# Linear attention with a gated feed-forward: activation tables chosen from sets, guard sums taken on VectorE, and a new order list

## The chip, the cores and the metric

The kernel runs on one core of a Trainium2 chip. The metric is the device time of one execution in microseconds (us). The engines of the core are TensorE (PE; its weight loads are shown apart as PEld), VectorE (DVE), ScalarE (ACT), GpSimd (POOL) and SyncE (SP, which here issues every DMA).

## The reference, cut to what matters

```
mag = sqrt(a_re² + a_im²);  scale = min(mag, 0.999) / (mag + 1e-6)
S[t] = (a[t]·scale[t]) * S[t-1] + k[t] v[t]^T        # complex decay per row of S, 48 x 48 a head
y[t] = q[t] · Re S[t]                                # 4 batches, 8 heads, 768 steps, 48 wide
x = y, heads side by side                            # 4 x 768 x 384
h = relu(x @ w_in)                                   # 384 -> 1024
c = sum over k of conv_w[k] * h shifted by k-1       # along the sequence, 3 taps
out = (h * sigmoid(c)) @ w_out                       # 1024 -> 384
```

## The kernel before, in words

The recurrence is rewritten as chunked attention. The sequence of each batch is cut into 6 chunks of 128 steps, 24 in all. Decays are summed as logarithms and phases along the sequence, so that q and k can be scaled by exp of the summed logarithm and turned by cosine and sine of the summed phase; what is left is a masked product of the two inside a chunk, and a state that is carried from chunk to chunk.

Work comes in 12 segments of two chunks. For each segment:

- `prelude` (L291) loads a_re and a_im (768 columns each) into the tile a_t, squares both on ACT (L300, L301, each with a sum along the row into one column of `gar` or `gai`), adds the squares on DVE (L302), takes logarithms and exponentials on ACT (L303 to L308), the quotient on DVE (L309), and a running sum on DVE (L312, three scans of 256). Then come the arctangent on ACT (L316), a running sum of the phase (L318, three scans), its turns as whole numbers (an ACT copy recorded at the helper's L281), their removal on DVE (L325) and an absolute value (L327).
- `products` (L329) loads q and k (tile qk_t) and v (v_t), takes two exponentials on ACT (L337, L338), scales k and q (L339, L340), takes cosine and sine on ACT (L344, L345; the function Sin), and multiplies on DVE (L346, L347, L348). The results are laid out head by head in two `stk` tiles by 16 DMAs (L353): eight from qk_t, which wait for L347, and eight from a_t, which wait for L348. SP issues them.
- For each chunk, `state` (L363) transposes on PE (L373), copies to `kn` on ACT (L374), multiplies (L380) and copies the state to `s_sb` (L387). `attention` (L390) computes scores on PE (L398), masks them on DVE (L401, tile p_t), and multiplies by state and values (L411). The result is copied to the tile `x` in two parts, on ACT (L423) and DVE (L424); a column at a unit's border is copied on ACT by `halo` (L431, recorded at L281).

The feed-forward works on 9 units of 256 or 384 steps, with four steps each of 256 hidden channels. `moe_front` (L464) has 18 matmuls into h_ps (L477), Relu on ACT (L480) and two convolution taps on DVE (L481, L483). `moe_back` (L486) has tanh on ACT (L495), the gate on DVE (L496), a two-part copy on ACT (L498) and DVE (L499), and the matmuls into o (L504); after the fourth step ACT copies o to os_t (L510) and SP stores it. At the start, w_in, w_out and conv_w arrive in a 64-bit layout and are turned into fp32 on DVE (L239 to L242), split into two parts on ACT (L272, L278) with PE's help (L276, L277).

At the end a few small DVE operations (L542 to L551) test the guard sums `gar` and `gai` against 4096 and other values against limits; where a limit is broken, a slow path (`recurrence`) runs. On these inputs it is not run.

The order of all of this is not left to the program text. `pieces` cuts the program into 1761 pieces (one instruction, or a run of PE instructions with the same target); `in_order` (L164) sorts them by the hand-written list `RANKS` (L45) and ties each engine's instructions into that one line. Each engine, and SP's queue, works strictly in that line's order. While it does so, it puts an activation table load (recorded at L181) in front of an ACT instruction whose function is not served by the table loaded last:

```
"Exp": (natural_log_exp,), "Ln": (natural_log_exp,), "Sin": (silu,), "Arctan": (sigmoid,), "Tanh": (sigmoid, silu)
need = table_of(row[0])
if need and table not in need:
    table = need[0]; row = [load of table, *row]
```

Squares, copies, Relu and Abs name no table and never cause a load.

Of the kernel before, what the change touches and what calls it, by code (L numbers as in the profile page):

```python
# [126 lines left out]
]  # L127

HINT = "TileBranchHintPlaceholder"
HINTED = {"EngineType.PE": 10, "EngineType.DVE": 1, "EngineType.Activation": 2, "EngineType.SP": 2, "EngineType.Pool": 0}  # L130

# [568 lines left out]
```

## Time and profile before

| what | us |
|---|---|
| median of 3 runs | 398.24 |
| lowest and highest | 397.48, 400.33 |
| the profiled execution's own time | 399.31 |
| its span, first to last instruction | 397.5 |
| ACT_TABLE_LOAD, 41 in all (40 of them by `in_order`) | 1.283 each |

The profile is of one execution. The span leaves out 1.8 us that lie around the instructions. Busy shares are of the span; a PE that is shown busy is not always at its peak, since its ends are modelled.

### The profile page before, as it was taken

What the parts mean: (1) busy time and instruction counts of PE and PEld (TensorE: products, weight loads), DVE (VectorE), ACT (ScalarE), POOL (GpSimd) and SP (SyncE); (2) the same over time, 40 slices, a digit from 0 to 9 for tenths busy, and PEclk for the clock granted to TensorE, in tenths of its full rate; (3) what the DMA queues carried; (4) which work ended last, traced back from release to release, by engine and by line L of the source; (5) the groups of instructions that cost most, each with busy time, mean ns of one, the idle gap of its engine ahead of it and who ended that gap; (6) DMA issues with size and microseconds to landing.
All of it is one profiled execution on the core that took longest, in us unless ns stands there. A gap on an engine that the chain in (4) does not pass through costs nothing. (4 is left out here: it accounts for less than half of the span.)

```text
span 397.5 us, 10141 instructions
## 1 busy us (share of the span) xinstructions
PE 359.7 (90%) x4146; PEld 326.6 (82%) x4146; DVE 334.6 (84%) x505; ACT 342.8 (86%) x602; POOL 4.0 (1%) x33
## 2 busy tenths in 40 slices
PE   1455696999999999999999989999999999999994
PEld 1123365899999999999989979999999999999994
DVE  3799976799999999999989977989999877862880
ACT  4999998899999999999998989999999887640751
POOL 2000000000000000000000000000000000000000
PEclk9997579799999999999999999999999999999999
DMA  8983678258774754692468823852718605500102
GB/s 300 419 326 103 103 170 224 91 119 195 201 184 147 146 145 120 130 228 75 89 103 239 190 96 101 145 193 87 137 25 183 164 2 103 119 2 2 59 0 70
DMA packets 31495, 55.03 MB, mean 138 GB/s; under 512 B 4304, under 2 KB 25808, under 8 KB 31440
## 3 DMA queue, kind: packets, MB, share of 16 engines
q1 hardware_dynamic: 31440, 54.31, 52.6%
q8 instruction: 34, 0.56, 0.6%
q14 instruction: 21, 0.17, 0.1%
HBM read 30.70 MB, written 4.72 MB: 89 GB/s over the span
## 5 line engine op out<-in xcount | busy, mean ns | idle before, releaser
L504 PE MATMUL o<-wo,hg 128*128 128x384 f32 x576 | 116.0, 345 | 0.0
L477 PE MATMUL h_ps<-x,wi 128*128 128x386 f32 (+1 forms) x648 | 113.0, 325 | 0.0
L477 PEld LDWEIGHTS h_ps<-x,wi 128*128 128x128 f32 x648 | 103.2, 189 | 1.7 <-issue 0.8
L504 PEld LDWEIGHTS o<-wo,hg 128*128 128x128 f32 x576 | 97.9, 188 | 2.6 <-issue 1.4
L398 PE MATMUL ps<-stk 96*128 96x128 f32 x384 | 52.4, 286 | 1.9 <-DMA stk<-a_t 1.7
L398 PEld LDWEIGHTS ps<-stk 96*128 96x128 f32 x384 | 49.7, 200 | 4.0 <-issue 2.7
L181 ACT ACT_TABLE_LOAD x40 | 51.3, 1283 | 0.7
L481 DVE SCALAR_TENSOR_TENSOR g_t<-h_t,cw 128x384 f32<-128x384 f32 (+1 forms) x72 | 39.9, 568 | 8.3 <-ACT h_t L480 8.0
L495 ACT ACTIVATE g_t<-g_t,cw 128x384 f32<-128x384 f32 (+1 forms) x72 | 39.5, 576 | 2.5 <-DVE g_t L483 2.5
L483 DVE SCALAR_TENSOR_TENSOR g_t<-h_t,cw,g_t 128x384 f32<-128x384 f32 (+1 forms) x72 | 39.5, 567 | 0.5
L480 ACT ACTIVATE h_t<-h_ps 128x386 f32<-128x386 f32 (+1 forms) x72 | 31.7, 452 | 8.8 <-PE h_ps L477 8.4
L401 DVE TENSOR_TENSOR p_t<-ps,mask 128x512 f32<-128x512 f32 x48 | 32.7, 683 | 6.9 <-PE ps L398 6.8
L276 PE MATMUL h_ps<-g_t,ident 128*128 128x384 f32 x32 | 21.9, 800 | 17.3 <-DVE g_t L242 9.6
L499 DVE TENSOR_TENSOR hg<-g_t,hg 128x768 fp32r<-128x768 f32 (+1 forms) x36 | 31.0, 862 | 5.5 <-ACT x L423 2.6
L496 DVE SCALAR_TENSOR_TENSOR g_t<-g_t,h_t 128x768 f32<-128x768 f32 (+1 forms) x36 | 30.7, 862 | 1.9 <-ACT g_t L495 1.8
L498 ACT ACTIVATE hg<-g_t 128x768 fp32r<-128x768 f32 (+1 forms) x36 | 27.7, 774 | 4.4 <-PE o L504 3.2
L276 PEld LDWEIGHTS h_ps<-g_t,ident 128*128 128x128 f32 x32 | 7.8, 285 | 24.1 <-issue 9.1
L411 PE MATMUL ps<-p_t,v_t 128*32 128x128 f32 x768 | 26.1, 273 | 0.0
L373 PE MATMUL ps<-ident,qk_t 128*128 128x128 f32 x120 | 20.4, 286 | 5.8 <-DVE x L424 3.4
L373 PEld LDWEIGHTS ps<-ident,qk_t 128*128 128x128 f32 x120 | 14.6, 144 | 10.0 <-DVE x L424 4.1
L411 PE MATMUL ps<-stk,s_sb 96*32 96x128 f32 x640 | 22.5, 281 | 0.0
L411 PEld LDWEIGHTS ps<-p_t,v_t 128*32 128x32 f32 x768 | 21.8, 109 | 0.9 <-issue 0.5
(96 smaller groups left out, 496.0 us busy)
## 6 DMA issues: line engine op xcount, KB each, us to landing
a_t<-in_a SPq DMA_DIRECT2D x12, 768.0 KB, 5.9
qk_t<-in_qk SPq DMA_DIRECT2D x12, 768.0 KB, 5.2
stk<-qk_t SPq DMA_DIRECT2D x96, 96.0 KB, 3.0
stk<-a_t SPq DMA_DIRECT2D x96, 96.0 KB, 3.0
v_t<-in_v SPq DMA_DIRECT2D x12, 448.0 KB, 3.6
out<-os_t SPq DMA_DIRECT2D x24, 192.0 KB, 3.1
stk<-in_w_in SPq DMA_DIRECT2D x4, 768.0 KB, 9.0
stk<-in_w_out SPq DMA_DIRECT2D x4, 768.0 KB, 7.4
```

Source lines behind the costliest of these rows:

```text
L181: row = [nc.scalar.preload_act_table_set(table).ins, *row]
L373: nc.tensor.transpose(tr[:, g - lo], kv[:, g // NG, g % NG], ident)
L398: nc.tensor.matmul(sp[:, h], lhsT=stk[0][:, hq * 4 + h], rhs=stk[1][:, hq * 4 + h], start=(h == 0), stop=(h == 3))
L401: nc.vector.tensor_tensor(out=p, in0=sp, in1=mask.unsqueeze(1).broadcast_to([128, 4, C]), op=ALU.mult)
L411: nc.tensor.matmul(yp[r0:r0 + 32, q // 4], lhsT=left[:, i, col:col + 32], rhs=right(h), start=r0 not in started, stop=n == len(sources) - ...
L477: nc.tensor.matmul(hp, lhsT=wi[:, f2, iw, i, kt], rhs=x[ix][:, kt], start=(k == 0), stop=(k == 8))
L480: nc.scalar.activation(h, hp, func=AF.Relu)
L481: nc.vector.scalar_tensor_tensor(out=g, in0=h[:, 0:n], scalar=cw[:, f, 0:1], in1=h[:, 1:n + 1], op0=ALU.mult, op1=ALU.add)
L483: nc.vector.scalar_tensor_tensor(out=g, in0=h[:, 2:n + 2], scalar=cw[:, f, 2:3], in1=g, op0=ALU.mult, op1=ALU.add)
L495: nc.scalar.activation(g[:, i], g[:, i], func=AF.Tanh, scale=cw[:, 2 * f2 + i, 1:2])
L499: nc.vector.tensor_tensor(out=lo, in0=g, in1=hi.bitcast(F32), op=ALU.subtract)
L504: nc.tensor.matmul(ops[t], lhsT=hg[:, k, t * C:(t + 1) * C], rhs=wo[:, f2, w, k], start=(f2 == 0 and hg is hi and k == 0 and w == 0), stop ...
```

## The change

A table of functions and of all tables that hold them takes the place of the old one. `in_order` now makes two passes over each line: in the first it keeps the set of tables that could serve every function met since the last load, narrows it with each function, and begins a new set only when none is left; in the second it puts in the loads. So the table of a load is picked by what comes after it, and arctangent and sine can share one (`trig_and_small`), as can exponential and tanh (`exp_and_others`).

The squares on ACT lose their row sums. The addition of the squares on DVE becomes a scalar_tensor_tensor that writes its own row sum, into one tile `gaa` where there were `gar` and `gai`. At the end one comparison and one reduction of 12 columns go. The list of 1761 numbers is replaced by one of 1759, with other numbers nearly throughout.

```diff
-TABLES = {"Exp": ("natural_log_exp_and_others",), "Ln": ("natural_log_exp_and_others",),
-          "Sin": ("silu_and_others",), "Arctan": ("sigmoid_and_others",),
-          "Tanh": ("sigmoid_and_others", "silu_and_others")}
+LOGEXP, EXP, SIGMOID, SILU, TRIG = ("natural_log_exp_and_others", "exp_and_others", "sigmoid_and_others",
+                                     "silu_and_others", "trig_and_small")
+TABLES = {"Ln": (LOGEXP,), "Exp": (LOGEXP, EXP), "Arctan": (TRIG, SIGMOID), "Sin": (TRIG, SILU),
+          "Tanh": (SIGMOID, SILU, EXP)}
...
-        last, table = None, None
-        for row in line:
-            need = table_of(row[0])
-            if need and table not in need:
-                table = need[0]
-                row = [nc.scalar.preload_act_table_set(table).ins, *row]
+        last, sets, loads = None, set(), {}
+        for k, row in enumerate(line):
+            need = set(table_of(row[0]) or ())
+            if need & sets:
+                sets &= need
+            elif need:
+                sets = loads[k] = need
+        for k, row in enumerate(line):
+            if k in loads:
+                row = [nc.scalar.preload_act_table_set(min(loads[k])).ins, *row]
...
-        nc.scalar.activation(r, u, func=AF.Square, accum_out=gar[:, p:p + 1])
-        nc.scalar.activation(e, t, func=AF.Square, accum_out=gai[:, p:p + 1])
-        nc.vector.tensor_tensor(out=r, in0=r, in1=e, op=ALU.add)
+        nc.scalar.activation(r, u, func=AF.Square)
+        nc.scalar.activation(e, t, func=AF.Square)
+        nc.vector.scalar_tensor_tensor(out=r, in0=r, scalar=1.0, in1=e, op0=ALU.mult, op1=ALU.add,
+                                       accum_out=gaa[:, p:p + 1])
...
-    for i, (x, lim) in enumerate(((gar, 4096.0), (gai, 4096.0), (gw.rearrange("p b g j -> p (b g j)"), 3600.0),
+    for i, (x, lim) in enumerate(((gaa, 4096.0), (gw.rearrange("p b g j -> p (b g j)"), 3600.0),
```

Laid against the program's pieces, the old list has 40 table loads among 537 ACT instructions, the new one 39 among the same 537. The first loads of the two lines, with the functions that each serves (L logarithm, E exponential, A arctangent, S sine, T tanh):

```
before  log-exp LLEELLEEL | sigmoid AA | silu SS | log-exp ELLEEE | silu SS | log-exp LEELELEL | sigmoid AA | log-exp EEL | silu SSSSTTTTTT
after   log-exp LELLE | trig A | log-exp EELLEE | trig ASS | log-exp LLEE | trig ASS | log-exp LEELLLEEE | trig ASS | log-exp ELLEELE | silu TTTSTSTT
```

## Rows read from the trace of the kernel before

**Rows 1.** The page: busy time, then PE and its granted clock in 40 slices.
```profile
PE 359.7 (90%) x4146; PEld 326.6 (82%) x4146; DVE 334.6 (84%) x505; ACT 342.8 (86%) x602; POOL 4.0 (1%) x33
...
PE   1455696999999999999999989999999999999994
...
PEclk9997579799999999999999999999999999999999
```

**Rows 2.** Windows: stretch, length; busy PE, PEld, DVE, ACT, POOL; PEclk, DMA share, GB/s.
```profile
0.00:60.00 60.00, 33.88 (x156) 18.73 (x157) 47.63 (x68) 53.26 (x84) 2.83 (x19) 0.83 0.74 237
...
30.00:40.00 10.00, 6.00 (x62) 3.62 (x60) 9.77 (x14) 9.94 (x15) 0.00 (x0) 0.71 0.41 106
...
60.00:80.00 20.00, 15.57 (x283) 13.85 (x282) 14.07 (x21) 17.62 (x33) 0.00 (x0) 0.83 0.57 158
...
68.40:75.20 6.80, 5.97 (x84) 5.72 (x88) 5.68 (x9) 5.61 (x10) 0.00 (x0) 0.50 0.53 184
...
80.00:300.00 220.00, 218.27 (x2724) 206.75 (x2724) 207.66 (x316) 213.22 (x385) 1.15 (x14) 1.00 0.58 140
```

**Rows 3.** Timeline of PE from 67 to 81 us: start, length, instructions, idle before and releaser.
```profile
67.52 0.44 PE L373 MATMUL ps<-ident,qk_t 128*128 128x128 f32 x2 [2.35 <-DVE x L424]
69.23 3.75 PE L398 MATMUL ps<-stk 96*128 96x128 f32 x16 [1.27 <-DMA stk<-a_t]
...
75.58 1.08 PE L411 MATMUL ps<-p_t,v_t 128*32 128x128 f32 x32
...
80.30 2.41 PE L477 MATMUL h_ps<-x,wi 128*128 128x258 f32 x18
```

**Rows 4.** Timeline of ACT, the first prelude and the copies of x.
```profile
8.13 0.19 ACT L300 ACTIVATION_READ_ACCUMULATOR a_t<-a_t 128x1 f32 x1
8.22 0.83 ACT L301 ACTIVATE e_t<-a_t 128x768 f32<-128x768 f32 x1
8.95 0.18 ACT L301 ACTIVATION_READ_ACCUMULATOR e_t<-a_t 128x1 f32 x1
9.16 1.28 ACT L181 ACT_TABLE_LOAD   x1
10.45 0.84 ACT L303 ACTIVATE a_t<-a_t 128x768 f32<-128x768 f32 x1
11.20 0.83 ACT L305 ACTIVATE a_t<-a_t 128x768 f32<-128x768 f32 x1
...
65.88 0.47 ACT L423 ACTIVATE x<-ps 128x384 fp32r<-128x384 f32 x1
...
76.73 0.49 ACT L423 ACTIVATE x<-ps 128x384 fp32r<-128x384 f32 x1 [0.20 <-PE ps L411]
```

**Rows 5.** Groups of ACT: what, count; busy us, mean ns; idle before.
```profile
L181 ACT ACT_TABLE_LOAD x40 | 51.3, 1283 | 0.7
...
L300 ACT ACTIVATION_READ_ACCUMULATOR a_t<-a_t 128x1 f32 x12 | 2.3, 195 | 0.0
```

**Rows 6.** Groups of DVE, the same columns.
```profile
L325 DVE SCALAR_TENSOR_TENSOR a_t<-a_t 128x768 f32<-128x768 f32 x12 | 11.4, 954 | 1.6 <-ACT a_t L281 1.5
L302 DVE TENSOR_TENSOR a_t<-a_t,e_t 128x768 f32<-128x768 f32 x12 | 11.4, 953 | 3.9 <-ACT e_t L301 3.9
...
L312 DVE TENSOR_TENSOR_SCAN a_t<-a_t,e_t 128x256 f32<-128x256 f32 x12 | 7.7, 676 | 0.0
```

**Rows 7.** Timeline of SP's queue around the transfers of segment 1.
```profile
52.26 1.85 SPq L353 DMA_DIRECT2D stk<-qk_t  x3
54.30 0.45 SPq L297 DMA_DIRECT2D a_t<-in_a  x1
...
59.30 2.97 SPq L353 DMA_DIRECT2D stk<-a_t  x3
62.37 0.54 SPq L335 DMA_DIRECT2D qk_t<-in_qk  x1
62.96 3.73 SPq L353 DMA_DIRECT2D stk<-a_t  x5
```

More of the change, by code (lines that the diff above doesn't have):

```diff
@@ L223, in linear_attention_moe_kernel @@
     cl = filled("cl", -L0, (128, B, NG, NC + 1))
-    gar = const.tile([128, len(segs)], F32, name="gar")
-    gai = const.tile([128, len(segs)], F32, name="gai")
+    gaa = const.tile([128, len(segs)], F32, name="gaa")
     gph = const.tile([128, len(segs), NG], F32, name="gph")
@@ L540, in linear_attention_moe_kernel @@
     gd = const.tile([128, B, NG, NC], F32, name="gd")
-    gb = const.tile([128, 5], F32, name="gb")
+    gb = const.tile([128, 4], F32, name="gb")
     nc.vector.tensor_tensor(out=gw, in0=cl, in1=cl, op=ALU.mult)
     nc.vector.tensor_tensor(out=gd, in0=cl[:, :, :, 1:NC + 1], in1=cl[:, :, :, 0:NC], op=ALU.subtract)
-    for i, (x, lim) in enumerate(((gar, 4096.0), (gai, 4096.0), (gw.rearrange("p b g j -> p (b g j)"), 3600.0),
+    for i, (x, lim) in enumerate(((gaa, 4096.0), (gw.rearrange("p b g j -> p (b g j)"), 3600.0),
                                   (gd.rearrange("p b g j -> p (b g j)"), 20.0),
```

161 rows, old and new, of the table RANKS are left out of this document.

## The prediction, made before the changed kernel ran

> **What bounds the kernel now.** I read the page first: the busy shares and the forty slices [rows 1]. PE is at 90% of the span, ACT at 86% and DVE at 84%, which by itself says little. The slices say more: PE climbs over the first eight and then stands at 9 or so to the end, and its granted clock falls below full speed only inside those eight. So I cut the span into stretches [rows 2]. From 80 to 300 us PE is busy 218.3 of 220 us, ACT 213.2 and DVE 207.7. All three are near full, but PE is the one without room: 1.7 us idle, against 6.8 for ACT and 12.3 for DVE. After 300 us ACT and DVE thin out in their own slices of the page, and PE stays full. What can be won behind 80 us by freeing ACT or DVE is therefore bounded by PE's idle time there, about 1.7 us.
>
> The first 80 us are another matter. Up to 60 us PE has only 33.9 us of work, while ACT is busy 53.3 and DVE 47.6 [rows 2], and from 30 to 40 us both are nearly full (9.94 and 9.77 of 10). Here the preludes and the weight conversion feed PE. From 60 to 80 us PE idles 4.4 us, and the last steps before the first feed-forward matmul at 80.30 can be followed one by one in PE's timeline [rows 3]: it waits 2.35 us for DVE's half of the copy of x of chunk 1, then 1.27 us for the stk transfers of segment 1, and runs chunk 2 from 69.23 to 76.7. [...] The copy of x of chunk 2 on ACT then starts at 76.73 with just 0.20 us idle in front of it [rows 4]. So there PE and ACT arrive together: ACT could have been there only 0.2 us sooner than PE let it.
>
> **The change part by part.** *Table loads.* The list of the change, laid against the program's pieces, gives 39 loads where there were 40. Pairing arctangent with sine is used early (four early loads serve A, then ASS three times), but these pairs do not lower the count much, since logarithms stand between them anyway. One load costs 1.283 us [rows 5] plus the overlap of neighbours that it breaks: without it, the logarithm at 10.45 would have followed the accumulator read at 8.95 by about 0.09 us, at 9.04, so 1.41 us in all [rows 4]. One load fewer: ACT -1.4 us.
>
> *Row sums off ACT.* Each square is now followed by an accumulator read, 24 in all, twelve behind L300 at 195 ns [rows 5] and twelve like them behind L301. Reads overlap their neighbours: the next square starts 0.09 us behind the read's start (8.13 to 8.22), so that is what each delays the line [rows 4]. 24 times 0.09 is 2.2 us. ACT in all: -3.6 us over the whole run.
>
> *Row sums onto DVE.* Twelve plain additions at 953 ns become twelve scalar_tensor_tensor with a sum. Without a sum that form takes 954 ns on the same shape, so the change of form costs nothing [rows 6]. No DVE instruction of this trace writes a row sum, so the sum is bounded. Below: the sum could come free with the addition, 0; a gain is excluded, since the same 768 pairs are read and written at the same pace. Above: the scan of 256 columns carries a value along its row and takes 676 ns [rows 6]; three of them, 2.03 us for 768 columns, are 1.07 us over the addition, 12.9 us for twelve. In between lies one more small instruction, as ACT has it: at that read's 195 ns [rows 5], twelve make 2.3 us. I take 2.3, since a separate read is what ACT's rows show for the same job. It stands beside DVE's 12.3 us of idle from 80 to 300 us and costs PE nothing there; where that cover is missing, at 20 to 50 us, two or three reads add under 0.5 us. The comparison and the reduction of 12 columns that go at the end lie beside a PE that is full up to the last slice [rows 1]: nothing.
>
> [...]
>
> *The new order.* This is the part that decides, since every ACT microsecond counts only where ACT's line, not PE's, comes last. I counted the ACT instructions ahead of two such places. Ahead of the copy of x of chunk 2, which lets the feed-forward begin, the old list has 91 instructions with 8 loads, the new one 94, also with 8. Five come in (three 768 wide, two of 3 columns), two 768 wide go out: one 0.75 us step (10.45 to 11.20) and two of about 0.1, together +0.95, less eight reads, 0.7 [rows 4]. That is +0.2 us. Ahead of the copy of x of chunk 21, late in the run, 477 with 38 loads become 480 with 39: three in (one 768, one 384 at the 0.47 us of the row at 65.88, one small) make +1.3, the load +1.4, 24 reads -2.2: +0.5 us. So what ACT saves is used to place other work earlier, and the places that PE waits for are not reached sooner.
>
> Small gains remain. In SP's queue the load of the next segment's q and k now stands behind the a_t transfers of segment 1, not between them, and 0.54 us of issue goes from that chain [rows 7]. On the other side, the load of segment 3's a stood behind three of segment 1's qk_t transfers and now stands ahead of all eight. It waits for a buffer that segment 0's own transfers must leave, and the eight are queued behind it: at worst the three that began at 52.26 wait until it went, at 54.30, 2.0 us [rows 7]; at best it goes before DVE has them ready. Since ACT's second sine of segment 1 is also one load and one instruction later in the new line, the transfers will hardly be ready at 52.26, and I take nothing for it. Half the scores of chunk 3 move behind the first feed-forward matmuls, which shifts PE's own work about and gains nothing. I take 1.0 us for the early part (0.54 from SP and some of the idle before 69.23) and 0.8, half of PE's 1.7 us, for 80 to 300.
>
> **Sum.** 399.31 (the profiled execution: span 397.5 and 1.8 around it) - 1.0 - 0.8 = 397.5. That execution is 1.07 above the median of the runs, so against the median the forecast is 396.4. A measurement of this kernel can tell about 1%, 4 us, from no change, so I call this the same.
>
> **The rivals.** *First, faster: the slow-clock stretch goes.* If chunk 2 reaches PE without the two waits, the drop at 68.4 need not come: its 5.97 us of PE work at 0.50 would take 3.0 [rows 2]. With half of the 4.4 us idle of 60 to 80 us and 1.0 of the 1.7 behind it, -6.2: 393.1, or 392.0 against the median. For it: the second sine of segment 0 is no longer the only hold on its a_t transfers, since the exponential of the same segment moves from 44th to 20th in ACT's line. Against it: ACT has as much work ahead of chunk 2's copy as before, and it was only 0.2 us early; idle that ACT spent waiting earlier in the ramp would have to go too.
>
> *Second, slower: DVE becomes the bound through its sums.* At the scan's pace each prelude gains 1.07 us on DVE. Three preludes lie in the stretch where DVE is full, +3.2 to the first matmul; eight more lie in 80 to 300, 8.6 us against 12.3 idle, of which I let a quarter show, +2.2. 399.31 + 5.4 = 404.7, or 403.6 against the median. It decides from about 0.5 us for each sum. Against it: the equal rows of the two forms [rows 6].
>
> *Third, slower: chunk 1's copy is late.* The new list puts it 83rd on ACT instead of 80th and behind one more table load, 7 instead of 6: five in (four of 768, one 384), two out (one of each), and that load, about +3.6, less eight reads, some 0.7: +2.9 on 65.88. PE's wait for x would end 2.9 us later, at 70.4; the scores then follow 0.4 us later at 70.9, not at 69.23: +1.6, and the longer idle could bring a second stretch of 6.8 us at half clock, +3.0. 403.9, or 402.8. It needs the earlier steps to gain nothing.
>
> *Fourth, the change does not do what it says.* Tables that the list pairs might still be loaded one by one; with 39 counted, even ten loads more would put 14 us on ACT, mostly in its 6.8 us of slack. I give this little.
>
> **How the numbers follow.** Forecast 0.57, clock rival 0.22, DVE rival 0.08, late copy 0.10, tables 0.03. Faster than 394.3: most of the clock rival and a little of the forecast, 0.23. Slower than 402.2: DVE rival, half of the late copy and the tables, 0.14. Same: 0.63. The range runs from just under the clock rival's 392.0 to about the late copy's 402.8: 391.5 to 402.5.
>
> **What would show it.** Right: 40 ACT_TABLE_LOADs in all, no accumulator reads on ACT, twelve sums on DVE at about 0.95 us each with a short read behind; first feed-forward matmul between 78 and 81 us; PE again over 218 of 220 us from 80 to 300. The clock rival shows as full clock from about 55 us on and a first matmul before 77. The DVE rival shows as additions of 1.5 us or more and PE waiting for DVE. The late copy shows as a PE wait for x that ends after 70 us. The forecast is wrong if PE's busy share behind 80 us moves by over 2 us in either direction.

## The result and the profile after

| | before | after |
|---|---|---|
| median of 7 runs each, us | 398.46 | 395.28 |
| lowest and highest | 397.48, 400.33 | 394.73, 397.06 |
| profiled execution: own time, span | 399.31, 397.5 | 395.28, 393.5 |

The ratio after to before is 0.9909, with a 95% interval of 0.9883 to 0.9935: 0.9% faster, or 3.2 us between the medians, and 4.0 us between the two profiled spans. The interval lies clear of no change, and on both sides of the 1% that the prediction set as its bound.

The page of the kernel after, the lines that answer to [rows 1]:

```profile
PE 353.5 (90%) x4146; PEld 323.6 (82%) x4146; DVE 334.5 (85%) x515; ACT 338.8 (86%) x577; POOL 3.8 (1%) x33
...
PE   1436678898999999999999999999999999999994
...
PEclk9999989999999999999999999999999999999999
```

Ahead of the last slice the granted clock is now under 1.00 in one slice only (0.83 from 49.19 to 59.02 us), and PE is busy 6.2 us less for the same 4146 matmuls. Matmuls showed longer at a lower granted clock: the 16 score matmuls of chunk 2 take 3.75 us in [rows 3], at 0.50 [rows 2], and 2.09 us further down, at 1.00. That is not the whole of it, since another execution of the kernel after (changed_again, below) has a mean clock of 0.965 and not 0.994, and its PE is busy 353.6 us all the same. Busy time over the whole span therefore does not measure work. Stretches at full clock, 1.00, measure it better. Of the kernel after, the windows that answer to [rows 2]:

```profile
0.00:60.00 60.00, 30.51 (x154) 17.91 (x154) 49.38 (x74) 53.96 (x79) 2.82 (x19) 0.97 0.74 233
60.00:80.00 20.00, 17.11 (x355) 15.25 (x355) 16.45 (x25) 19.94 (x38) 0.00 (x0) 1.00 0.81 212
80.00:300.00 220.00, 218.06 (x2676) 206.94 (x2675) 207.34 (x322) 212.86 (x371) 1.03 (x14) 1.00 0.60 139
```

Behind 80 us both kernels run at a granted clock of 1.00 until their last slice (0.93 in both), so PE's busy time from there on measures the work that is left. Before: 359.7 on the page less 33.88 and 15.57 in the windows, 310.2 us of work left, and 397.5 - 80 - 310.2 = 7.3 us of idle behind. After: 353.5 - 30.51 - 17.11 = 305.9 us left, and 7.6 us idle. **So the whole difference of 4 us is work that PE had done by 80 us; its idle behind 80 us is the same in sum.** The counts agree: behind 80 us the kernel after has 71 matmuls fewer (18 into h_ps, 48 of the state, 5 of scores), which the rows price at 2.41, 0.88 and some 0.6 us, 3.9 us in all. The idle is not the same in place, as windows of 20 us show. The kernel before, then the kernel after:

```profile
80.00:100.00 20.00, 19.97 (x283) 18.99 (x283) 19.47 (x34) 19.88 (x43) 0.20 (x2) 1.00 0.69 163
...
200.00:220.00 20.00, 19.57 (x215) 18.54 (x206) 18.66 (x26) 18.82 (x31) 0.00 (x0) 1.00 0.75 178
220.00:240.00 20.00, 18.74 (x312) 17.12 (x312) 16.55 (x26) 18.03 (x35) 0.13 (x2) 1.00 0.54 151
...
280.00:300.00 20.00, 20.00 (x190) 19.16 (x189) 19.77 (x32) 18.50 (x33) 0.13 (x2) 1.00 0.48 82
```

```profile
80.00:100.00 20.00, 18.82 (x283) 17.48 (x283) 18.37 (x33) 18.43 (x39) 0.16 (x2) 1.00 0.77 177
...
200.00:220.00 20.00, 20.00 (x245) 18.75 (x244) 19.18 (x29) 19.86 (x34) 0.13 (x2) 1.00 0.60 120
220.00:240.00 20.00, 20.00 (x322) 18.72 (x321) 18.32 (x26) 19.63 (x33) 0.00 (x0) 1.00 0.42 139
...
280.00:300.00 20.00, 19.23 (x185) 18.15 (x183) 18.05 (x26) 17.04 (x32) 0.13 (x2) 1.00 0.51 84
```

The kernel after gives back 1.15 us at 80 to 100 us and 0.77 at 280 to 300; the kernel before loses 1.69 at 200 to 240 us, where the kernel after loses nothing.

**How the first 80 us were won.** ACT's timeline of the kernel before, from 20 to 80 us, has five instructions with idle in front, together 3.05 us. Four of them (the fifth is the copy at 76.73 in [rows 4]):

```profile
27.77 0.87 ACT L278 ACTIVATE wi<-h_ps 128x384 fp32r<-128x384 f32 x2 [0.54 <-PE h_ps L277]
56.71 0.49 ACT L278 ACTIVATE wo<-h_ps 128x384 fp32r<-128x384 f32 x1 [0.26 <-PE h_ps L277]
61.91 0.85 ACT L300 ACTIVATE a_t<-a_t 128x768 f32<-128x768 f32 x1 [0.90 <-DMA stk<-a_t]
74.48 0.47 ACT L387 COPY s_sb<-s_ps 96x384 f32<-96x384 f32 x1 [1.15 <-PE s_ps L380]
```

In the kernel after, ACT's timeline has no such row between 20 and 80 us. Its copy of x of chunk 2 starts at 73.11, not at 76.73, 3.62 us earlier:

```profile
60.49 0.87 ACT L304 ACTIVATE a_t<-a_t 128x768 f32<-128x768 f32 x1
...
66.47 0.50 ACT L428 ACTIVATE x<-ps 128x384 fp32r<-128x384 f32 x1
...
73.11 0.48 ACT L428 ACTIVATE x<-ps 128x384 fp32r<-128x384 f32 x1
```

The windows from 20 us to that copy say which kind of time went, before and after:

```profile
20.00:76.73 56.73, 40.87 (x410) 28.12 (x411) 49.15 (x64) 53.42 (x89) 0.00 (x0) 0.76 0.64 177
```

```profile
20.00:73.11 53.11, 36.16 (x413) 25.33 (x413) 48.53 (x66) 52.96 (x85) 0.00 (x0) 0.97 0.72 187
```

ACT's work up to the copy is 0.46 us less, its idle 0.15 us instead of 3.31. The longest wait of the preludes, at 61.91, is that of segment 3's first square. The profile puts it down to a stk transfer, but its input is the load that SP issued at 54.30 behind three transfers of segment 1 [rows 7]; that one landed 7.4 us later, at 61.7. In the kernel after SP's queue has the load four microseconds earlier, ahead of all eight transfers (six in the row below, two at 62.95). It landed 4.3 us later, at 54.7, and the square runs at 60.49 without a wait:

```profile
50.35 0.35 SPq L301 DMA_DIRECT2D a_t<-in_a  x1
55.25 3.77 SPq L358 DMA_DIRECT2D stk<-qk_t  x6
```

PE's timeline after, against [rows 3], has 2.89 us of waits from 60 to 80 us where the kernel before had 4.43, and then feed-forward matmuls that stand between the two halves of a chunk's scores:

```profile
67.51 0.44 PE L378 MATMUL ps<-ident,qk_t 128*128 128x128 f32 x2 [1.56 <-ACT kn L379]
67.78 2.09 PE L403 MATMUL ps<-stk 96*128 96x128 f32 x16
...
74.13 0.44 PE L378 MATMUL ps<-ident,qk_t 128*128 128x128 f32 x2 [1.08 <-ACT kn L379]
74.82 1.16 PE L403 MATMUL ps<-stk 96*128 96x128 f32 x8 [0.25 <-DVE x L429]
75.74 2.41 PE L482 MATMUL h_ps<-x,wi 128*128 128x258 f32 x18
```

**The stall at 235 us.** In the kernel before, ACT stands 1.86 us before the square of a late prelude, whose load SP issued at 224.30 and which landed 6.7 us later, at 231.0 (the row says "issue", a wait for nothing that the profile shows). The prelude's table load and logarithm then lie ahead of the copy `kn`, and PE waits for that:

```profile
224.30 0.33 SPq L297 DMA_DIRECT2D a_t<-in_a  x1
...
231.25 0.84 ACT L300 ACTIVATE a_t<-a_t 128x768 f32<-128x768 f32 x1 [1.86 <-issue]
...
232.21 1.28 ACT L181 ACT_TABLE_LOAD   x1
...
234.73 0.58 ACT L374 COPY kn<-ps 128x512 f32<-128x512 f32 x1
...
235.36 0.44 PE L373 MATMUL ps<-ident,qk_t 128*128 128x128 f32 x2 [1.26 <-ACT kn L374]
```

In the kernel after, that segment's load goes at 219.89, no first square of a prelude stands near, and the six transposes are one group without a wait:

```profile
219.89 0.33 SPq L301 DMA_DIRECT2D a_t<-in_a  x1
...
231.10 0.82 PE L378 MATMUL ps<-ident,qk_t 128*128 128x128 f32 x6
```

PE's timeline of the kernel after has three waits behind 80 us: 0.36 and 0.69 us for stk transfers of a_t near 90 us, and one for ACT:

```profile
300.08 3.39 PE L509 MATMUL o<-wo,hg 128*128 128x384 f32 x18 [0.85 <-ACT os_t L515]
```

Last, the groups of the kernel after that answer to [rows 5, 6]:

```profile
L186 ACT ACT_TABLE_LOAD x39 | 50.0, 1283 | 0.6
...
L306 DVE SCALAR_TENSOR_TENSOR a_t<-a_t,e_t 128x768 f32<-128x768 f32 x12 | 11.4, 949 | 1.3 <-ACT a_t L304 1.2
...
L306 DVE DVE_READ_ACCUMULATOR a_t<-a_t,e_t 128x1 f32 x12 | 1.0, 82 | 0.0
```

### The profile page after: what moved, and what is told of

Same layout as the page of the kernel before. It is cut to its first block, busy times and chain, and to the rows that moved or that the text cites. A ratio compares the mean times of both kernels' runs of the same rounds, so it can differ in the third digit from the quotient of the medians.

```text
span 393.5 us, 10104 instructions
## 1 busy us (share of the span) xinstructions
PE 353.5 (90%) x4146; PEld 323.6 (82%) x4146; DVE 334.5 (85%) x515; ACT 338.8 (86%) x577; POOL 3.8 (1%) x33
## 5 line engine op out<-in xcount | busy, mean ns | idle before, releaser
L482 PE MATMUL h_ps<-x,wi 128*128 128x386 f32 (+1 forms) x648 | 111.7, 324 | 0.1
L403 PE MATMUL ps<-stk 96*128 96x128 f32 x384 | 50.9, 282 | 1.3 <-DMA stk<-a_t 1.0
L403 PEld LDWEIGHTS ps<-stk 96*128 96x128 f32 x384 | 48.1, 196 | 3.6 <-issue 1.4
L186 ACT ACT_TABLE_LOAD x39 | 50.0, 1283 | 0.6
L280 PE MATMUL h_ps<-g_t,ident 128*128 128x384 f32 x32 | 20.0, 736 | 28.4 <-DVE g_t L246 11.7
L353 DVE TENSOR_TENSOR a_t<-a_t 128x1536 f32<-128x1536 f32 x12 | 21.0, 1752 | 0.1
```

The lines of the kernel that those rows point to most:

```text
L186: row = [nc.scalar.preload_act_table_set(min(loads[k])).ins, *row]
L403: nc.tensor.matmul(sp[:, h], lhsT=stk[0][:, hq * 4 + h], rhs=stk[1][:, hq * 4 + h], start=(h == 0), stop=(h == 3))
L482: nc.tensor.matmul(hp, lhsT=wi[:, f2, iw, i, kt], rhs=x[ix][:, kt], start=(k == 0), stop=(k == 8))
```

## The experiments

Two theories stood at first: that the new order of the ramp (the part up to the first feed-forward matmul) brings the gain, R in the texts below, and that the ACT work which the tables and sums save brings it, W. Ratios are to the kernel before on the same chip; its median was 399.27 us for the first four, 400.07 for the next four and 399.48 for the last four. For the profiled execution of each, the table gives PE's work left at 80 us and its idle behind, worked out as above. These are of one execution each, up to 2.0 us off the kernel's median (tables_only: 402.20 against 400.17), so differences of a microsecond in them are rough. In order_and_sums the granted clock also falls behind 80 us (0.99 from 80 to 300 us, where each of the others has 1.00), so its work left contains some of that.

| kernel | median | ratio (95%) | span | work left | idle behind 80 |
|---|---|---|---|---|---|
| before | 398.46 | | 397.5 | 310.2 | 7.3 |
| after | 395.28 | 0.9909 (0.9883 to 0.9935) | 393.5 | 305.9 | 7.6 |
| changed_again | 395.79 | 0.9892 (0.9861 to 0.9923) | 393.7 | 306.2 | 7.5 |
| sums_only | 399.68 | 1.0005 (0.9977 to 1.0034) | 398.3 | 310.1 | 8.3 |
| tables_only | 400.17 | 1.0013 (0.9981 to 1.0045) | 400.5 | 312.2 | 8.3 |
| order_and_sums | 408.75 | 1.0223 (1.0174 to 1.0272) | 407.2 | 314.2 | 13.0 |
| order_and_tables | 397.32 | 0.9945 (0.9916 to 0.9974) | 395.9 | 307.5 | 8.4 |
| new_early | 398.95 | 0.9973 (0.9946 to 1.0000) | 397.9 | 308.9 | 9.0 |
| old_early | 402.25 | 1.0049 (1.0017 to 1.0081) | 401.4 | 311.4 | 10.0 |
| filled_waits | 399.18 | 0.9969 (0.9942 to 0.9996) | 398.8 | 309.7 | 9.1 |
| sum_apart | 399.52 | 0.9992 (0.9970 to 1.0013) | 396.7 | 308.6 | 8.1 |
| small_on_pool | 395.01 | 0.9882 (0.9853 to 0.9911) | 393.2 | 305.8 | 7.4 |
| square_on_pool | 398.63 | 0.9977 (0.9947 to 1.0007) | 396.1 | 308.2 | 7.9 |
| small_on_pool_before | 402.60 | 1.0082 (1.0048 to 1.0117) | 400.1 | 312.0 | 8.1 |

**sums_only.** The kernel before with the sums moved to DVE; its own list, with the two end operations on the sums placed behind the last of them.

```diff
-        nc.scalar.activation(r, u, func=AF.Square, accum_out=gar[:, p:p + 1])
...
-        nc.vector.tensor_tensor(out=r, in0=r, in1=e, op=ALU.add)
+        nc.scalar.activation(r, u, func=AF.Square)
...
+        nc.vector.scalar_tensor_tensor(out=r, in0=r, scalar=1.0, in1=e, op0=ALU.mult, op1=ALU.add,
+                                       accum_out=gaa[:, p:p + 1])
```

> The old list and the old table rule, with only the guard sums moved to VectorE (its two end tests go behind the last sum). Theory R (the gain is made before the first feed-forward matmul, mostly by the granted clock staying up while chunk 2 runs): ACT's line is 2.2 us shorter over the run, but only 0.7 us of it ahead of the copy of x of chunk 2, where PE came last by 0.2 us; so 397.5 to 398.5 us, ratio 0.997 to 1.000. Theory W (ACT's line is the bound and every microsecond taken off it counts): 24 reads of 0.09 us, -2.2 us, 396.2 us, ratio 0.9945.

No difference; W's 0.9945 lies outside the interval. What ACT saved became a longer wait at the same place of the same list, in ACT's timeline of this run:

```profile
62.00 0.84 ACT L298 ACTIVATE a_t<-a_t 128x768 f32<-128x768 f32 x1 [1.81 <-DMA stk<-a_t]
```

The square starts at 62.00, as before at 61.91, with 1.81 us idle in front of it and not 0.90: it is tied to its load, which SP issued at 54.08 here and which landed 7.7 us later, at 61.8. Saved ACT time was worth nothing so long as that load kept its place in SP's queue.

**tables_only.** The kernel before with the new table rule alone: 38 loads where there were 40.

```diff
-TABLES = {"Exp": ("natural_log_exp_and_others",), "Ln": ("natural_log_exp_and_others",),
...
+TABLES = {"Ln": (LOGEXP,), "Exp": (LOGEXP, EXP), "Arctan": (TRIG, SIGMOID), "Sin": (TRIG, SILU),
```

> The old list and sums on ACT, with only the new table rule: 38 loads instead of 40. One of the two that go stands in the ramp (arctangent and sine of segment 0 share a table), one near the end, where ACT has room. Theory R: the ramp load puts ACT 1.4 us ahead before the first transfers of segment 0, of which the wait for transfers and for PE leaves a part: -0.5 to -1.4 us, ratio 0.9965 to 0.999, and more (to 0.990) only if the granted clock then stays up through chunk 2. Theory W: two loads, -2.8 us, 395.6 us, ratio 0.993.

No difference either; W's 0.993 lies outside the interval. The same square stands at 61.90 in its trace, and ACT's idle between 20 us and the copy of x of chunk 2 is 5.41 us, where it was 3.05: a load less became more waiting.

**order_and_sums.** The kernel after with the table rule of before, so that its list has 49 loads and not 39.

```diff
-TABLES = {"Ln": (LOGEXP,), "Exp": (LOGEXP, EXP), "Arctan": (TRIG, SIGMOID), "Sin": (TRIG, SILU),
...
+TABLES = {"Exp": ("natural_log_exp_and_others",), "Ln": ("natural_log_exp_and_others",),
```

> The new list with sums on VectorE, but the old table rule: 49 loads instead of 39, of which 11 instead of 8 lie ahead of the copy of x of chunk 2. Theory R: the three loads in the ramp count in full, +4.2 us on the changed kernel, and the seven others are partly covered by ACT's idle time behind 80 us (about 7 us): 400 to 404 us, ratio 1.004 to 1.014. Theory W: ten loads of 1.4 us, +14 us, 409 us, ratio 1.027. If neither: the list does not depend on the table rule and the time stays at 395.

Slower than the kernel before and the kernel after, between R (1.014 at most) and W (1.027). Against the kernel after it is 0.0314 of 399.3, 12.5 us, for ten loads of 1.283 us. Its group of loads and its window behind 80 us:

```profile
L181 ACT ACT_TABLE_LOAD x49 | 62.9, 1283 | 0.8
```

```profile
80.00:300.00 220.00, 215.28 (x2668) 202.96 (x2666) 202.40 (x313) 216.79 (x369) 0.90 (x12) 0.99 0.60 140
```

ACT is full at 216.8 of 220, and PE's idle has grown to 4.7 us there. So ten loads that the new list was not laid for count nearly in full, 12.5 of 12.8 us.

**order_and_tables.** The kernel after with the row sums on ACT again.

```diff
-        nc.vector.scalar_tensor_tensor(out=r, in0=r, scalar=1.0, in1=e, op0=ALU.mult, op1=ALU.add,
...
+        nc.scalar.activation(r, u, func=AF.Square, accum_out=gar[:, p:p + 1])
```

> The new list and the new table rule, with the guard sums back on ACT: 24 accumulator reads on ACT again, none on VectorE. Theory R: eight reads ahead of chunk 2's copy, 0.7 us, and little behind: 395.3 to 396.3 us, ratio 0.992 to 0.9945. Theory W: +2.2 us, 397.5 us, ratio 0.9975.

Under the new list the sums are worth 0.9945 - 0.9909 of 399, 1.4 us, against nothing under the old one; the two intervals overlap, so the size is rough. It is at the upper end of R's range, and W's 0.9975 lies just outside the interval. The copy of x of chunk 2 comes at 74.12, 1.0 us later than in the kernel after, and ACT has no idle row between 20 us and that copy in either. The order with its tables keeps the larger part.

**new_early and old_early.** Both have the tables and sums of the kernel after. The first takes the new list up to the first feed-forward matmul and the old one behind it, the second the reverse. Each engine's line is joined at that time, and the numbers of the list follow from it.

```diff
 RANKS = (
...
-    83, 45, 87, 48, 90, 46, 79, 47, 80, 49, 94, 85, 84, 86, 96, 98, 50, 95, 51, 100, 56, 106,
+    83, 45, 87, 48, 90, 46, 79, 47, 80, 49, 94, 85, 84, 86, 96, 98, 50, 95, 51, 101, 60, 118,
...
```

> The changed kernel, but only the part of the list up to the first feed-forward matmul is the new one (the first 99 ACT, 88 DVE, 53 PE, 53 SP pieces of the lines); behind it all pieces stand in the old list's order. Table rule and sums as changed. Theory R (the gain is made before the first feed-forward matmul and carried to the end): 395 to 396.5 us, ratio 0.990 to 0.994. Theory L (the later part of the new list makes it, by a better order for PE): 398 to 400, ratio 0.998 to 1.003. The last runs showed that ACT's line counts almost in full under the new list, so how ACT's loads fall behind the first 99 pieces may matter too: if old order behind new costs loads, it lies above both.

> The mirror: the old list up to its first feed-forward matmul at 80.3 us, the new list behind it, table rule and sums as changed. Theory R: the first feed-forward matmul at 79 to 81 us and 397.5 to 400 us, ratio 0.997 to 1.003. Theory L: 394.5 to 396.5, ratio 0.989 to 0.994.

Neither half has the gain, so R (first half) and L (second half) both miss. With the new ramp and the old rest, 1.4 us less work is left at 80 us than before, and 1.8 us more idle stands behind it; among it is the old list's stall, smaller but still there:

```profile
235.00 0.44 PE L378 MATMUL ps<-ident,qk_t 128*128 128x128 f32 x2 [0.54 <-ACT kn L379]
```

Its ramp did come sooner: the copy of x of chunk 2 starts at 74.13, 2.60 us ahead of the kernel before, and the first feed-forward matmul at 78.43. So the earlier copy by itself is not the gain.

With the old ramp and the new rest it is slower than before: 1.1 us more work is left at 80 us and 2.7 us more idle follows. Between the halves lies the interleaving of the first feed-forward steps with chunk 3, which neither hybrid has whole; how much of the miss is the seam itself is not parted here.

**filled_waits.** The kernel before, with ten and five further matmuls on PE in its two waits ahead of chunk 2. Nothing reads their result.

```diff
+        if c == 2:
+            for count in (10, 5):
+                fill = psH.tile([128, 512], F32, name="h_ps")[:, 0:128]
+                for _ in range(count):
+                    nc.tensor.matmul(fill, lhsT=ident, rhs=mask, start=True, stop=True)
```

> The kernel before, with ten fp32 matmuls of 128 columns put into PE's first wait ahead of chunk 2 (2.35 us) and five into its second (1.27 us); their result is read by nobody. If the idle of these two waits is what lets the granted clock fall for chunk 2, and the clock is what costs, the clock stays at 1.00 from about 55 us on, the first feed-forward matmul moves from 80.3 to 77 to 78 us, and the run takes 395.5 to 397 us, ratio 0.991 to 0.995. If the earlier order of ACT, DVE and SP is what moves it (rival), the time stays within 0.3% of before, or rises by up to 0.5 us for the added matmuls. If the clock stays up and the time does not move, ACT was the bound there all along.

Over 68.4 to 75.2 us the clock stayed at 1.00, against 0.50 in [rows 2]:

```profile
68.40:75.20 6.80, 6.03 (x140) 5.31 (x138) 5.38 (x10) 6.76 (x11) 0.00 (x0) 1.00 0.57 186
```

ACT's waits at 74.48 and 76.73 are gone in this trace, and the copy of x of chunk 2 starts 1.48 us sooner than before:

```profile
75.25 0.48 ACT L428 ACTIVATE x<-ps 128x384 fp32r<-128x384 f32 x1
```

The first feed-forward matmul came at 78.81 instead of 80.30, but 1.9 us more idle followed behind 80 us in this execution, which was 1.4 us above the kernel's median; over its runs the kernel is 0.3% faster (0.6% at most by the interval). The slow stretch was worth little by itself.

**sum_apart.** The kernel after with the addition and a separate reduction on DVE.

```diff
+        nc.vector.tensor_tensor(out=r, in0=r, in1=e, op=ALU.add)
+        nc.vector.tensor_reduce(out=gaa[:, p:p + 1], in_=r, axis=mybir.AxisListType.X, op=ALU.add)
```

> The changed kernel, with the row sum taken by a separate reduction on VectorE (768 columns, about 0.9 us each, twelve of them) behind a plain addition, in place of the sum inside the addition. It measures what DVE time costs under the new list. If DVE has room, as its 12 us of idle behind 80 us would say, only the three or four in the ramp count, of which ACT's next logarithm waits for one: +0.9 to +3 us on the changed kernel, ratio 0.993 to 0.9985. If DVE is as close to the bound as ACT proved to be: +11 us, ratio 1.018.

```profile
L308 DVE TENSOR_REDUCE gaa<-a_t 128x1 f32<-128x768 f32 x12 | 11.4, 953 | 0.4
```

The reductions are 11.4 us where the kernel after has 1.0 us of reads, and DVE is busy 9.6 us more on the page (344.1 against 334.5). That cost 0.9992 - 0.9909, 0.8% or 3.3 us: nearly the whole gain. DVE has no room for a second pass over the data; that the 1.0 us of reads costs nothing was not measured by itself.

**changed_again.** The kernel after, unchanged, on the chip of the last four.

> The changed kernel itself, beside the three others on the same chip: 0.988 to 0.994 of the kernel before, as measured first.

As fast as the first time, though its profiled execution had a granted clock of 0.83 over the first 80 us, where that of after had 0.98. Late in the ramp it lost the clock where after kept it, as the same window of the two shows:

```profile
69.00:72.40 3.40, 3.40 (x73) 3.12 (x76) 2.82 (x5) 3.00 (x5) 0.00 (x0) 0.51 1.02 404
```

```profile
69.00:72.40 3.40, 3.40 (x121) 3.08 (x120) 2.95 (x5) 3.37 (x5) 0.00 (x0) 1.00 1.01 408
```

Two waits for PE, of 0.37 and 0.42 us, now stand ahead of its copy of x of chunk 2, which comes 0.89 us later than in the profiled execution of after:

```profile
74.00 0.49 ACT L428 ACTIVATE x<-ps 128x384 fp32r<-128x384 f32 x1 [0.42 <-PE ps L416]
```

Its first feed-forward matmul came at 76.36, 0.6 us later, and its execution took 395.47 against 395.28 us.

**small_on_pool, square_on_pool, small_on_pool_before.** If ACT's line counts, work taken off it should help. The first moves the 44 small copies (into `cl`, `gph` and across the borders of x) from ACT to GpSimd in the kernel after; the second moves the twelve second squares there too; the third does the first's edit in the kernel before.

```diff
+    def pool_copy(dst, src, scale=None):
+        if scale is None:
+            nc.gpsimd.tensor_copy(dst, src)
+        else:
+            nc.gpsimd.tensor_scalar(dst, src, scale, None, op0=ALU.mult)
...
-        nc.scalar.activation(e, t, func=AF.Square)
+        nc.gpsimd.tensor_tensor(out=e, in0=t, in1=t, op=ALU.mult)
```

> The changed kernel with the 44 smallest ACT copies (12 of cl, 12 of gph, 20 of a border column of x, 3 or 6 columns each) done by GpSimd, which is idle; nothing else in the lines moves. Each takes about 0.1 us of ACT's line, 4.4 us in all. Theory A (under the new list ACT's line is what binds: ten loads of 1.4 us cost 13 us, 24 reads of 0.09 us some 1.4): -2.9 to -4.2 us on the changed kernel, ratio to the kernel before 0.980 to 0.985. Theory P (PE binds behind 80 us, ACT's time counts only when it is added): 0 to -1 us, ratio 0.988 to 0.991. If GpSimd's hand-overs to ACT, DVE and PE are slow, it comes out above the changed kernel.

> As the run with 44 copies on GpSimd, and the second of the two squares of each prelude on GpSimd too (12 of 128x768, 0.73 us of ACT's line each, 8.8 us). Theory A: another -5 to -8 us, ratio 0.962 to 0.972, if GpSimd's square is done before DVE's addition needs it. Theory P: as with the copies alone. If GpSimd takes several us for a square, the addition waits in each prelude, and in the ramp that shows at once: +2 us or more.

> The kernel before (old list, old tables, sums on ACT) with the same 44 copies on GpSimd: 4.4 us off ACT's line. If ACT's line binds there as well: -2.9 to -4.2 us, ratio 0.989 to 0.993. If the old list is held by other things in its ramp, as the run with the sums alone (2.2 us off ACT, no change) says: within 0.3% of before.

The first has the lowest median of the study, 0.8 us under changed_again on the same chip, and its interval overlaps that one's: a gain is not shown. ACT is busy 335.7 us on its page, against 338.8 in the kernel after: 3.1 us saved, and theory A's 2.9 to 4.2 us did not follow. Theory P's 0.988 to 0.991 holds. The other two are slower than the kernels that they start from. Groups of the first, and one of the second:

```profile
L289 POOL CAST x<-x 128x3 fp32r<-128x3 f32 x20 | 10.1, 512 | 50.6 <-ACT x L434 37.2 <-DVE x L435 12.8 <-DMA stk<-qk_t 0.5
L289 POOL COPY cl<-a_t 128x6 f32<-128x6 f32 x12 | 8.6, 720 | 193.8 <-ACT kn L385 53.5 <-DVE a_t L323 23.3 <-ACT hg L510 22.4
```

```profile
L311 POOL TENSOR_TENSOR e_t<-a_t 128x768 f32<-128x768 f32 x12 | 21.6, 1804 | 86.1 <-ACT a_t L315 24.3 <-ACT hg L510 22.8 <-DMA stk<-a_t 19.7
```

A copy of three columns takes 512 ns there and 206 on ACT in the kernel after, a square 1804 ns and 843 on ACT. The work is off ACT's line, but its result comes later: in square_on_pool ACT has 3.81 us of idle between 20 us and the copy of x of chunk 2, most of it in waits for DVE, where the kernel after has none. That this delay is the whole cause of the lost time is not shown.

## Why the prediction came out as it did

The forecast of 396.4 us was 1.1 us above the 395.28 measured, and "the same" holds by the bound that it set, narrowly. Its sum was 1.8 us of gain; the medians differ by 3.2 and the profiled spans by 4.0. That the total came so near owes something to luck: the early part was taken too small and the part behind 80 us too large. One sum does not come out: the chances of being slower add up to 0.16 from their parts (0.08, 0.05 and 0.03), not 0.14. Step by step:

- *Table loads, 40 in all, at 1.283 us*: as forecast (39 and the first).
- *Sums on DVE, 2.3 us*: mis-sized. An addition with a sum takes 949 ns, where the plain one takes 953 [rows 6], and its read 82, 1.0 us for twelve, where ACT's row was the model. The DVE rival fell with it, but its price was of the right size: it held 12.9 us more on DVE to cost 5.4, and sum_apart shows 3.3 for 9.6.
- *"The places that PE waits for are not reached sooner"*: this is the step that failed. The count of ACT's work ahead of the copy of x of chunk 2 was good (+0.2 us forecast; 0.46 less measured from 20 us on), but the copy came 3.62 us sooner, because 3.2 us of ACT's idle ahead of it went. The sum read the 0.20 us in front of that copy as ACT's whole room; the waits at 61.91 and 74.48 further up the same line were room too, since everything behind them moves when they go. The prediction names that idle only as a condition of its clock rival.
- *The load of segment 3's a, "I take nothing for it"*: weighed for the transfers queued behind it alone. Its own reader was left out: the square that had waited for it no longer waits. How much of the gain that is, no run shows.
- *Early part, 1.0 us*: mis-sized. The work left at 80 us is 4.3 us less, of which the next 20 us give back 1.15.
- *80 to 300 us, 0.8 us*: PE is busy 218.06 us there, within the 2 us either way that was asked, and 0.2 less than before, not 0.8 more. Nearly all of the old idle did go, 1.69 of 1.73 us, that of 200 to 240 us, but 1.9 us of new idle at 80 to 100 and 280 to 300 us took its place.
- *Ten loads more "mostly in its 6.8 us of slack"*: wrong. order_and_sums shows them at 12.5 us. ACT's 6.8 us of idle are not slack that can be spent anywhere, and 12.8 us would not fit in it.
- *Late copy of chunk 1*: it came at 66.47, 0.59 us later than before and not 2.9; 1.70 us of the same idle (27.77, 56.71 and 61.91) was missing from this count.
- *The clock rival*: its signs partly came true. First feed-forward matmul at 75.74, under its 77 and outside the forecast's 78 to 81, and a clock of 1.00 from 54.2 us to the last slice in the profiled execution. Its price did not: filled_waits kept the clock at 1.00 over that stretch for 0.3%, and changed_again, at 0.51 from 69.0 to 72.4 us, was as fast as the kernel after. Part of ACT's vanished idle goes with the clock all the same: the waits at 74.48 and 76.73 are gone in filled_waits too, 1.35 of the 3.05 us, and the copy came 1.48 of the 3.62 us sooner there. The rest, the waits at 27.77, 56.71 and 61.91, stands in filled_waits at 1.70 us as before, and is gone in the kernel after.

What stays open: how the gain parts between the load's earlier place, the other moves of the list, and the tables that the list was laid for. The list was not run with that one load put back, and the old list was not run with tables and sums together. new_early shows that a copy of x 2.60 us sooner does not make the gain where the old order follows, so the account of the ramp is read from the traces and not proven by a run.

## What to carry to other kernels

When an order changes, count the idle ahead of a deadline as well as the work ahead of it: each wait on the bounding line can go (3.31 us became 0.15 here), and the instruction that follows it shows which queue decides that. Saved work was worth nothing on a line that stands at a late load (sums_only, ratio 1.0005). Added work cost nearly its full length on a line that hardly waits (order_and_sums, 12.5 us for 12.8), but 3.1 us taken off that same line brought no gain that is clear of noise (small_on_pool). So what adding costs does not tell what saving brings, and a cheaper operation and the order made for it are to be measured together. To see where a gain lies, compare the work that the bounding engine has left at one time, at full clock, and its idle behind that time.

## What the runs showed of the hardware that was not expected

- DVE's read of a row sum took 82 ns, ACT's 195 [rows 5], and the sum itself added nothing to a 768-column scalar_tensor_tensor (949 ns with it, 954 without [rows 6]).
- Two executions of one kernel, with a wait of PE of 1.54 and 1.56 us at 67 us, had granted clocks of 0.51 and 1.00 over 69.0 to 72.4 us. So the wait in front of the stretch did not by itself decide that the clock falls, as the prediction's clock rival had it. What decides it is not shown; the two clocks had differed before, too (over the first 60 us, some 0.80 against 0.97; the 0.80 is an estimate from 0.83 over the first 80 us and 0.51 over this stretch).
- One load serves arctangent and sine here: behind the one at 30.59 us, arctangent runs at 31.88 and the function Sin at 32.63 and 35.76, and the next load stands at 37.33. It takes the same 1283 ns as every other.
